# Values, up and down loaded in fewer or differently cut transfers at the end of a decode step

## The chip, the core and the metric

The kernel runs on one core of one Trainium2 chip. The metric is the device time of one execution in microseconds. Five engines work beside each other, each through its own queue of instructions in order: TensorE (PE: matmuls, and PEld: the loads of its stationary operand), VectorE (DVE), ScalarE (ACT), GpSimd (POOL) and SyncE (SP), which here does nothing but issue transfers from main memory. Sixteen DMA engines carry those out.

## What is computed

One decode step of a transformer block, for a single token of width 640, with 32 heads of 128 and a cache of 16384 positions per head:

```
mod = silu(c) @ w_mod                       # sa, ca, ga, sb, cb, gb: 640 each
h = layernorm(x) * (1 + ca) + sa
q = h @ wq                                  # 32 heads of 128
p = softmax(q . k_cache / sqrt(128))        # per head, over 16384 positions
x = x + ga * ((p . v_cache) @ wo)
h = layernorm(x) * (1 + cb) + sb
x = x + gb * ((silu(h @ w_gate) * (h @ w_up)) @ w_down)     # 640 -> 1728 -> 640
```

All inputs are bf16. The two caches are 128 MiB each in bf16, so nearly all of the bytes are keys and values.

## The kernel before

**Heads in pairs.** The 32 heads go as 16 pairs. A pair's keys (8192 KB) lie in one half of `kring`, 64 KB in each of 128 partitions; its values lie in `vbuf`, only the last pair's values in the first half of `kring` (`v_at`, line 482). VectorE multiplies keys by the query and folds the products (lines 540 to 562), TensorE adds up the rest against an identity matrix (line 530, or 570 for the first and last pair), ScalarE takes exponentials (588), and TensorE multiplies by the values (504, one matmul per four positions of a partition).

**Transfers.** `dma` (line 79) puts a transfer on SyncE's queue; SyncE issues it when its dependencies are met, in program order. Within a transfer each partition's bytes are one contiguous run of main memory. A later step waits for a transfer by name. The lists of cut points say how a tensor is divided into transfers, and the steps that use it are divided at the same points: `VCUT` for the last pair's values (line 481; used in `load_v` and `pv`), `WCUT` for wo's heads (625; used in the transfers and in `project`), `UK` for w_up's five slices (638; steps `up0` and `up1`), and `NB` blocks of 512 rows, plus a short one, for w_down (227 and 642).

**The tail.** After the last pair's scores (`o_R[15]`) the second half of `kring` is free, and w_gate, w_up and w_down are loaded there, in this order, behind the last values and wo, which went out earlier. On TensorE, in this order, stand: the last pair's exponentials' sum, its values (`pv`, `diag`), the heads' column form (`am`), wo (670), the columns (682), the second layer norm's two sums (380, 389) with gate's first slice between them, gate's other four slices (`gate`), a row form of x (726), up (704 again), and down (751). Between them VectorE and ScalarE do the small steps: layer norm, silu, the product gate x up (`gu`, line 740), and after down the last two operations (755, 756) and two stores.

**Columns of gate and up, rows of down.** w_down's 1728 rows are spread over partitions, so that one matmul contracts 128 of them. In a block of 512 rows, partition p holds rows 4p to 4p + 3: chunk j of the block is every fourth row. The short block has 192 rows on 96 partitions, two each. Gate's and up's outputs must stand in that same order. `chunk(j)` gives for each of the 14 chunks the columns of w_gate and w_up, a slice with that step, and `f_gu` (line 699) loads them as the stationary operand of a matmul with a moving operand of one or two columns: 14 matmuls per slice of 128 inputs, 70 for up and 70 for gate.

```
def chunk(j):
    return (slice(512 * (j // 4) + j % 4, 512 * (j // 4) + 512, 4), 128) if j < 4 * NB else (slice(512 * NB + j % 4, F, 2), FR)
...
last = e.matmul(ps_t[0:w, n * j:n * j + n], lhsT=wv[:, k, cols], rhs=src[:, n * k:n * k + n], ...)
```

Down takes the 14 chunks in order, four matmuls each (one for each quarter of the 640 outputs, side by side in the array), and accumulates all in one bank: the first chunk starts the sum, the last stops it. Each of the four `down` steps waits for the product `gu` and for its own transfer.

Of the kernel before, what the change touches and what calls it, by code (L numbers as in the profile page):

```python
# [37 lines left out]
class _Plan:  # L38
# [34 lines left out]
    def op(self, eng, fn, deps=(), name="", chan=None):  # L73
        o = _Op(eng, fn, list(deps), name, len(self.ops), self.loop.get(eng), chan)
        o.sig = chan is not None
        self.ops.append(o)
        return o

    def dma(self, out_ap, in_ap, key, deps=(), name="", eng="sp", noncontig=False):
        nc = self.nc  # L80

        def fn(e, out_ap=out_ap, in_ap=in_ap, noncontig=noncontig):
            if noncontig:
                with nc.allow_non_contiguous_dma(reason="tiny vector layout change"):
                    return e.dma_start(out_ap, in_ap)
            return e.dma_start(out_ap, in_ap)  # L86

        return self.op(eng, fn, deps, name, chan=self.dma_chan(key))
# [126 lines left out]
def build(nc, A_x, A_k, A_v, A_wq, A_wo, B_wg, B_wu, B_wd, c_in, w_mod, out):  # L215
    H, S, Dh = A_k.shape[1], A_k.shape[2], A_k.shape[3]
    D = A_x.shape[2]
    F = B_wg.shape[1]
    assert Dh == 128 and D % 128 == 0 and S == 128 * 128 and H == 32
    KC = D // 128  # L220
    NP = H // 2
    T2 = 2 * S // 128
    NCH = T2 // 4
    SCALE = float(Dh) ** -0.5
    EPS = 1e-5
    NB = F // 512
    FT = F - 512 * NB
    assert FT % 2 == 0 and FT // 2 <= 128
    FR = FT // 2
    FCH = 4 * NB + 2  # L230
    QW = 32
    QR = 16
    RW = D // 4
# [3 lines left out]
    with es:  # L237
        block = es.enter_context(nc.Block())
        plan = _Plan(nc, es)
        op, dma = plan.op, plan.dma  # L240
        POOL, ACT, DVE, PE = "pool", "act", "dve", "pe"

        def sb(name, shape, dtype):
            return es.enter_context(nc.sbuf_tensor(name, list(shape), dtype))
# [10 lines left out]
        wu_v = kb[:, KC * F:2 * KC * F].rearrange("p (k n) -> p k n", k=KC)  # L255
        wd_v = kb[:, 2 * KC * F:2 * KC * F + FCH * D].rearrange("p (k n) -> p k n", k=FCH)

# [40 lines left out]
        h2_col = sb("h2_col", [128, KC], BF16)  # L298
        ab = sb("ab", [128, KC, 2], BF16)
        g_sb = sb("g_sb", [128, FCH], F32)  # L300
        eg = sb("eg", [128, FCH], F32)
        dg = sb("dg", [128, FCH], F32)
        rg = sb("rg", [128, FCH], F32)
        sg = sb("sg", [128, FCH], F32)
        gu_col = sb("gu_col", [128, FCH], BF16)
# [22 lines left out]
        u_ps = psb[1]  # L328
# [101 lines left out]
        def pick(half, n, o_m, free):  # L430
# [14 lines left out]
            deps=[o_m0, o_xn], name="t1")  # L445
# [11 lines left out]
        for g in range(H // 4):  # L457
            b = g % 2
# [9 lines left out]
            for half in range(2):  # L468
# [4 lines left out]
                    deps=[o_q[g]], name="qbc%d_%d" % (g, half)))  # L473
# [4 lines left out]
        d_k, d_v = [None] * NP, [None] * NP  # L478
        o_R, o_pv, o_exp, o_nb, o_mx, o_acc, o_ot = ([None] * NP for _ in range(7))
        KCUT = [0, T2 // 2, T2]  # L480
        VCUT = [0, 3 * T2 // 4, T2]
        v_at = lambda p: vbuf[:] if p < NP - 1 else kring[:, 0]

        def load_k(p):
# [5 lines left out]
        def load_v(p):  # L490
            deps = [o_R[NP - 2]] if p == NP - 1 else [o_pv[p - 1]] if p >= 1 else [o_q[-1]]
            cuts = VCUT if p == NP - 1 else [0, T2]
            d_v[p] = [dma(v_at(p)[:, a:b, :], v_src(p)[:, a:b, :], ("v", p == NP - 1, c), deps=deps, name="dma_v%d_%d" % (p, c))
                      for c, (a, b) in enumerate(zip(cuts, cuts[1:]))]

        def pv(p):
            cuts = VCUT if p == NP - 1 else [0, T2]
            prev = None
# [54 lines left out]
        def score_end(p, c, between=None):  # L553

            kv = kring[:, p % 2, KCUT[c]:KCUT[c + 1]]
            o = op(DVE, lambda e: e.tensor_tensor(  # L556
                out=kv, in0=kv, in1=qbc[:, p, :].unsqueeze(1).broadcast_to([128, KCUT[c + 1] - KCUT[c], 128]), op=ALU.mult),
                deps=[d_k[p][min(c, len(d_k[p]) - 1)]] + o_qev[p // 2], name="mult%d_%d" % (p, c))
            for i, w in enumerate((64, 32, 16)):
                if between and i < 2:  # L560
                    between[i]()
                o = op(DVE, lambda e, w=w: e.tensor_tensor(out=kv[:, :, 0:w], in0=kv[:, :, 0:w], in1=kv[:, :, w:2 * w], op=ALU.add),  # L562
                       deps=[o], name="fold%d_%d_%d" % (p, c, w))
            return o
# [43 lines left out]
        for p in range(1, NP - 1):  # L608
            plan.in_loop(("pe",), "pairs", (p - 1) // 2, NLOOP)
            if p >= FIRST:  # L610
# [8 lines left out]
        PL = NP - 1  # L619
        load_v(PL)  # L620
        f0 = score_end(PL, 0, before(PL))
        reduce_end(PL, 0, f0)
        pv(PL - 1)
        wo_src = A_wo.rearrange("(p k) n -> p k n", p=128)
        WCUT = [0, H // 2, 7 * H // 8, H]
        d_wo = [dma(wo_v[:, a:b, :], wo_src[:, a:b, :], ("wo", a), deps=[o_pv[PL - 1]], name="dma_wo%d" % a) for a, b in zip(WCUT, WCUT[1:])]
        diag(PL - 1)
        f1 = score_end(PL, 1)
# [6 lines left out]
        wdeps = [o_R[NP - 1]]  # L635
        d_wg = dma(wg_v, B_wg.rearrange("(p k) n -> p k n", p=128), "wg", deps=wdeps, name="dma_wg")
        wu_src = B_wu.rearrange("(p k) n -> p k n", p=128)
        UK = KC - 1
        d_wu = [dma(wu_v[:, 0:UK, :], wu_src[:, 0:UK, :], "wu0", deps=wdeps, name="dma_wu0"),
                dma(wu_v[:, UK:KC, :], wu_src[:, UK:KC, :], "wu1", deps=wdeps, name="dma_wu1")]  # L640
        d_wd = []
        for b in range(NB):
            d_wd.append(dma(wd_v[:, 4 * b:4 * b + 4, :].rearrange("p r n -> p (r n)"),
                            B_wd[512 * b:512 * b + 512, :].rearrange("(p r) n -> p (r n)", r=4), ("wd", b), deps=wdeps, name="dma_wd%d" % b))
        d_wd.append(dma(wd_v[0:FR, 4 * NB:FCH, :].rearrange("p r n -> p (r n)"),
                        B_wd[512 * NB:F, :].rearrange("(p r) n -> p (r n)", r=2), ("wd", NB), deps=wdeps, name="dma_wd%d" % NB))

# [1 line left out]
                 deps=[o_exp[PL], o_rz, o_onesf, o_rstd], name="L")  # L651
# [8 lines left out]
                  deps=[o_z, o_e32] + o_qev[-2], name="am")  # L660
        o_as = op(ACT, lambda e: e.activation(out=A_sb[:], in_=A_ps[:, 0:H], func=ACTF.Copy), deps=[o_am], name="as")

        def project(c):

            def f_wo(e):
                last = None
                for k in range(WCUT[c], WCUT[c + 1]):
                    r = k % 4
# [4 lines left out]
            return op(PE, f_wo, deps=[o_as, d_wo[c], o_exp[NP - 2]] + o_qev[-1], name="wo%d" % c)  # L673
        for c in range(len(WCUT) - 1):
            o_p = project(c)
        o_wr = [op(ACT, lambda e, a=a, b=b, ps=ps: e.activation(out=wo_row[:, a:b], in_=ps[:, 0:b - a], func=ACTF.Copy),
                   deps=[o_p, f1], name="wo_row%d" % a) for ps, a, b in ((wr_ps[0], 0, 512), (wr_ps[1], 512, D))]

        def f_cols(e):
# [9 lines left out]
        o_zu = op(DVE, lambda e: e.memset(u_ps[:, 0:FCH], 0.0), deps=[o_exp[NP - 1]], name="zero_u")  # L689
# [4 lines left out]
            deps=[o_ga, o_xf], name="x1")  # L694

        def chunk(j):
            return (slice(512 * (j // 4) + j % 4, 512 * (j // 4) + 512, 4), 128) if j < 4 * NB else (slice(512 * NB + j % 4, F, 2), FR)

        def f_gu(e, wv, ps_t, src, n, k0, k1):
            last = None  # L700
            for k in range(k0, k1):
                for j in range(FCH):
                    cols, w = chunk(j)
                    last = e.matmul(ps_t[0:w, n * j:n * j + n], lhsT=wv[:, k, cols], rhs=src[:, n * k:n * k + n],
                                    start=(k == 0 and j == 0), stop=(k == KC - 1 and j == FCH - 1), skip_group_check=True)
            return last
# [3 lines left out]
        def gate0(o_xc1):  # L710
# [6 lines left out]
            deps=[o_xc1, o_rstd1, o_onep_b], name="t2")  # L717
        o_h2 = op(DVE, lambda e: e.tensor_tensor(out=h2_col[:], in0=tt3[:], in1=sb_, op=ALU.add), deps=[o_t2], name="h2_col")
# [9 lines left out]
            return last  # L728
        o_xr = op(PE, f_xr, deps=[o_xsp, o_ot[PL], o_msk], name="x1_rows")
        o_x1r = op(ACT, lambda e: e.activation(out=x1_row, in_=xr_ps[:, 0:RW], func=ACTF.Copy), deps=[o_xr], name="x1_row")  # L730
        o_u0 = op(PE, lambda e: f_gu(e, wu_v, u_ps, h2_col, 1, 0, UK), deps=[o_h2, d_wu[0], o_zu], name="up0")
        o_u = op(PE, lambda e: f_gu(e, wu_v, u_ps, h2_col, 1, UK, KC), deps=[o_h2, d_wu[1], o_u0], name="up1")
        gp = g_ps[:, 0:2 * FCH].rearrange("p (j n) -> p j n", n=2)
        o_gt = op(DVE, lambda e: e.tensor_scalar_mul(out=sg[:], in0=gp[:, :, 0], scalar1=st[:, 7:8]), deps=[o_g, o_rstd1], name="gate_r")
        o_gs = op(DVE, lambda e: e.tensor_tensor(out=g_sb[:], in0=gp[:, :, 1], in1=sg[:], op=ALU.add), deps=[o_gt], name="gate_s")
# [4 lines left out]
        o_gum = op(DVE, lambda e: e.tensor_tensor(out=gu_col[:], in0=u_ps[:, 0:FCH], in1=sg[:], op=ALU.mult), deps=[o_sg, o_u], name="gu")  # L740

        prev = None
        for b in range(NB + 1):
            js = list(range(4 * b, min(4 * b + 4, FCH)))

            def f_down(e, b=b, js=js):
                last = None
                for j in js:
                    w = chunk(j)[1]
                    for r in range(4):  # L750
                        last = e.matmul(f_ps[32 * r:32 * r + 32, 0:RW], lhsT=wide(gu_col[0:w, j:j + 1]), rhs=wd_v[0:w, j, RW * r:RW * r + RW],  # L751
                                        start=(j == 0), stop=(j == FCH - 1), tile_position=(0, 32 * r))
                return last
            prev = op(PE, f_down, deps=[o_gum, d_wd[b], prev, o_nb[PL]], name="down%d" % b)
        o_t3 = op(DVE, lambda e: e.tensor_tensor(out=tt_row, in0=f_ps[:, 0:RW], in1=gb_row[:], op=ALU.mult), deps=[prev, o_gb], name="gb_ffn")
        o_or = op(DVE, lambda e: e.tensor_tensor(out=o_row[:], in0=tt_row, in1=x1_row, op=ALU.add), deps=[o_t3, o_x1r], name="o_row")
        o_dst = out[0, 0].rearrange("(r n) -> r n", r=4)
# [51 lines left out]
```

## Time and profile before

| | us |
|---|---|
| time, median of 3 runs | 681.06 (680.71 to 681.47) |
| the profiled execution's own time | 680.78 |
| its span, first to last instruction | 679.0 |
| TensorE busy | 365.4 (54%) |
| VectorE busy | 512.4 (75%) |
| ScalarE busy | 46.7 (7%) |
| main memory read | 290.47 MB, 428 GB/s over the span |

The profile is of one execution. Its instructions carry the number of the source line that issued them, the engine, the tensors written and read, their shape, and in brackets how long the engine had been idle before and what ended that. In such a row the first number is the start in microseconds from the start of the span, the second the time until the last of the merged instructions ends. In rows about a transfer the last number is the time from its issue by SyncE to the landing of its last byte. A window's row gives its bounds and length, the busy time and the count for PE and PEld, the share of full clock that TensorE was granted, the transfers' busy share and their rate.

### The profile page before, as it was taken

The numbers are of one execution on the slowest core, as the hardware profiler recorded it, in microseconds if no ns is written. First come the engines' busy times: TensorE is split into PE (matmuls) and PEld (weight loads), VectorE is DVE, ScalarE is ACT, GpSimd is POOL, SyncE is SP. The second block draws the span as 40 slices with busy tenths as digits, with TensorE's granted clock in tenths as the row PEclk, the third lists the DMA queues.
The fourth block names the chain that finished last, engine by engine and source line by source line (L and its number), as shares of the span: only waits on it lengthen the run. The fifth ranks groups of instructions, "written<-read, shape, count | busy, mean of one in ns | idle before, by whom it ended". The sixth has DMA issues, their size and how long they took to land.

```text
span 679.0 us, 4923 instructions
## 1 busy us (share of the span) xinstructions
PE 365.4 (54%) x2075; PEld 143.7 (21%) x2075; DVE 512.4 (75%) x181; ACT 46.7 (7%) x147; POOL 0.7 (0%) x6
## 2 busy tenths in 40 slices
PE   2522284755638174754818275663718475571666
PEld 1111122221212122221302122221212222121236
DVE  2189997959596996959597895959598695959801
ACT  1120000100000000000000010000000000000010
POOL 0000000000000000000000000000000000000000
PEclk9675565655657575565757555575756556575775
DMA  8999999999999999999999999999999999999997
GB/s 374 441 460 432 432 432 430 432 429 432 432 429 432 440 432 432 432 432 432 436 432 432 432 432 432 432 436 432 432 432 432 432 432 432 432 433 431 415 432 289
DMA packets 6612, 290.59 MB, mean 428 GB/s; under 512 B 746, under 2 KB 748, under 8 KB 1484
## 3 DMA queue, kind: packets, MB, share of 16 engines
q1 hardware_dynamic: 6596, 290.48, 99.2%
q8 instruction: 6, 0.10, 0.1%
q14 instruction: 2, 0.02, 0.0%
q10 hardware_dynamic: 8, 0.00, 0.0%
HBM read 290.47 MB, written 0.00 MB: 428 GB/s over the span
## 4 chain that ended last, share of the span: by engine, by line
DMA 49%; DVE 30%; issue 12%; PE 8%; SPq 0%; DVEq 0%
DMA kring<-in_A_k_cache_dram 45%; DVE kring L540 10%; PE psb L530 7%; DVE kring L545 6%; DVE kring L556 5%; DVE kring L562 5%; DMA kring<-in_B_w_down_dram 4%; DVE kring L550 3%; PE psb L570 1%; SPq L86 0%; DVE pm L576 0%; DVE nb L584 0%; PE psb L751 0%; DVEq L187 0%; DVEq L540 0%
## 5 line engine op out<-in xcount | busy, mean ns | idle before, releaser
L540 DVE TENSOR_TENSOR kring<-kring,qbc 128x16384 bf16<-128x16384 bf16 x28 | 243.2, 8687 | 96.3 <-DMA kring<-in_A_k_cache_dram 96.3
L530 PE MATMUL psb<-kring,ident 128*128 128x256 bf16 x448 | 197.4, 607 | 119.2 <-DVE kring L550 119.2
L545 DVE TENSOR_TENSOR kring<-kring 128x8192 bf16<-128x8192 bf16 x28 | 123.7, 4420 | 0.5
L530 PEld LDWEIGHTS psb<-kring,ident 128*128 128x128 bf16 x448 | 51.7, 121 | 249.1 <-DVE kring L550 128.8
L504 PE MATMUL psb<-vbuf,PZ 128*8 128x512 bf16 x960 | 82.0, 516 | 0.0
L580 PE MATMUL psb<-d,bd_f 128*128 128x64 f32 x32 | 11.0, 447 | 122.7 <-ACT d L578 122.7
L550 DVE TENSOR_TENSOR kring<-kring 128x4096 bf16<-128x4096 bf16 x28 | 64.0, 2285 | 0.5
L556 DVE TENSOR_TENSOR kring<-kring,qbc 128x16384 bf16<-128x16384 bf16 x4 | 34.8, 8688 | 23.5 <-DMA kring<-in_A_k_cache_dram 23.5
L504 PEld LDWEIGHTS psb<-vbuf,PZ 128*8 128x8 bf16 x960 | 26.5, 109 | 60.1 <-issue 50.9
L570 PE MATMUL psb<-kring,ident 128*128 128x128 bf16 x64 | 14.5, 392 | 40.5 <-DVE kring L562 40.5
L580 PEld LDWEIGHTS psb<-d,bd_f 128*128 128x128 f32 x32 | 8.0, 311 | 124.9 <-ACT d L578 66.5
L562 DVE TENSOR_TENSOR kring<-kring 128x8192 bf16<-128x8192 bf16 (+2 forms) x12 | 31.7, 2644 | 0.3
L519 PEld LDWEIGHTS psb<-sel,acc_sb 128*128 128x128 f32 x128 | 28.5, 310 | 8.4 <-issue 4.3
L519 PE MATMUL psb<-sel,acc_sb 128*128 128x2 f32 x128 | 25.6, 322 | 1.4 <-ACT acc_sb L510 1.4
L510 ACT ACTIVATE acc_sb<-psb 128x512 f32<-128x512 f32 x16 | 9.6, 597 | 206.1 <-PE psb L504 206.1
L588 ACT ACTIVATE PZ<-psb,nb 64x256 bf16<-64x256 f32 x32 | 15.0, 469 | 64.8 <-DVE nb L584 64.6
L570 PEld LDWEIGHTS psb<-kring,ident 128*128 128x128 bf16 x64 | 7.4, 122 | 46.9 <-DVE kring L562 41.8
L578 ACT ACTIVATE d<-negid,pm 128x64 f32<-128x64 f32 x16 | 5.6, 348 | 155.5 <-DVE pm L576 155.5
L463 PE MATMUL psb<-vbuf,h_col 128*128 128x512 bf16 x40 | 11.6, 463 | 7.9 <-DMA vbuf<-in_A_wq_dram 7.9
L523 ACT ACTIVATE OT_sb<-psb 128x2 f32 (+1 forms) x16 | 2.8, 172 | 155.7 <-PE psb L519 155.7
L576 DVE TENSOR_REDUCE pm<-psb 128x1 f32<-128x256 f32 x16 | 6.7, 417 | 3.7 <-PE psb L570 3.7
L463 PEld LDWEIGHTS psb<-vbuf,h_col 128*128 128x128 bf16 x40 | 4.3, 116 | 15.5 <-DMA vbuf<-in_A_wq_dram 8.8
(96 smaller groups left out, 78.6 us busy)
## 6 DMA issues: line engine op xcount, KB each, us to landing
kring<-in_A_k_cache_dram SPq DMA_DIRECT2D x2, 4096.0 KB, 40.1
kring<-in_A_v_cache_dram SPq DMA_DIRECT2D x1, 6144.0 KB, 34.1
vbuf<-in_A_wq_dram SPq DMA_DIRECT2D x1, 5120.0 KB, 25.6
kring<-in_w_mod_dram SPq DMA_DIRECT2D x1, 4800.0 KB, 14.0
vbuf<-in_A_wo_dram SPq DMA_DIRECT2D x1, 2560.0 KB, 18.7
kring<-in_B_w_gate_dram SPq DMA_DIRECT2D x1, 2160.0 KB, 18.9
kring<-in_A_v_cache_dram SPq DMA_DIRECT2D x1, 2048.0 KB, 38.7
vbuf<-in_A_wo_dram SPq DMA_DIRECT2D x1, 1920.0 KB, 23.0
```

The lines of the kernel that those rows point to most:

```text
L463: last = e.matmul(q_ps[b][:, 0:512], lhsT=h_col[:, k:k + 1].broadcast_to([128, 128]), rhs=wq_v[:, k, g * 512:(g + 1) * 512], start=(k == 0 ...
L504: last = e.matmul(acc_ps[32 * s:32 * s + 8, :], lhsT=PZ[:, p % 2, j, :], rhs=v_at(p)[:, 4 * j:4 * j + 4, :].rearrange("p t d -> p (t d)"), ...
L519: last = e.matmul(OT_ps[:, 0:2], lhsT=acc_sb[:, 128 * i:128 * (i + 1)], rhs=sel[:, i:8:4], start=(i == 0), stop=(i == 3))
L530: last = e.matmul(S_ps[p % 2][:, 0:T2], lhsT=ident[:], rhs=kring[:, p % 2, :, d], start=(d == 0), stop=(d == QW + QR - 1))
L540: return e.tensor_tensor(out=kv4, in0=kv4, in1=q4, op=ALU.mult)
L545: o_f = op(DVE, lambda e: e.tensor_tensor(out=kv4[:, :, 0], in0=kv4[:, :, 0], in1=kv4[:, :, 1], op=ALU.add), deps=[o_m], name="fold%d_%d" ...
L550: return op(DVE, lambda e: e.tensor_tensor(out=lo[:, :, 0:QR], in0=lo[:, :, 0:QR], in1=lo[:, :, QR:QW], op=ALU.add), deps=[o_f], name="fol ...
L556: o = op(DVE, lambda e: e.tensor_tensor(out=kv, in0=kv, in1=qbc[:, p, :].unsqueeze(1).broadcast_to([128, KCUT[c + 1] - KCUT[c], 128]), op= ...
L562: o = op(DVE, lambda e, w=w: e.tensor_tensor(out=kv[:, :, 0:w], in0=kv[:, :, 0:w], in1=kv[:, :, w:2 * w], op=ALU.add), deps=[o], name="fol ...
L570: last = e.matmul(S_ps[p % 2][:, KCUT[c]:KCUT[c + 1]], lhsT=ident[:], rhs=kring[:, p % 2, KCUT[c]:KCUT[c + 1], d], start=(d == 0), stop=(d ...
L580: o_mx[p] = op(PE, lambda e: e.matmul(mx_ps[:, 0:64], lhsT=bd_f[:], rhs=d2[:], start=True, stop=True), deps=[o_d2, o_bd1, o_bd2, o_nb[p - ...
L588: o_exp[p] = op(ACT, lambda e, half=half, ps=ps: e.activation(out=PZ[ps, p % 2, :, 4 * half:4 * half + 4], in_=S_ps[p % 2][ps, 0:T2].rearr ...
```

## The change

Five lists are cut differently.

- The last pair's values go in one transfer in place of two (three quarters and one quarter), and their product in one step.
- wo goes in two transfers, 28 heads and 4, in place of three (16, 12 and 4).
- w_up goes in one transfer in place of two (four slices and one), and `up0` and `up1` become one step.
- w_down's blocks become: rows 0 to 1023 with 8 to a partition, rows 1536 to 1727 with 2 to each of 96 partitions, and rows 1024 to 1535 with 4 to a partition, in this order of chunks.
- w_down's transfers stay four: the whole first block, the whole short block, and the last block's first three rows of each partition and then its fourth. Down's steps follow: 8, 2, 3 and 1 chunks.

```
-    NB = F // 512
-    FT = F - 512 * NB
-    FCH = 4 * NB + 2
+    FT = F % 512
+    FR = FT // 2
+    FCH = 14
+    BLOCKS = [(0, 128, 8, 0), (1536, FR, 2, 8), (1024, 128, 4, 10)]
+    DOWN = [(0, 0, 8), (1, 0, 2), (2, 0, 3), (2, 3, 4)]
...
-        VCUT = [0, 3 * T2 // 4, T2]
+        VCUT = [0, T2]
...
-        WCUT = [0, H // 2, 7 * H // 8, H]
+        WCUT = [0, 7 * H // 8, H]
...
-        UK = KC - 1
-        d_wu = [dma(wu_v[:, 0:UK, :], wu_src[:, 0:UK, :], "wu0", deps=wdeps, name="dma_wu0"),
-                dma(wu_v[:, UK:KC, :], wu_src[:, UK:KC, :], "wu1", deps=wdeps, name="dma_wu1")]
+        d_wu = dma(wu_v, wu_src, "wu", deps=wdeps, name="dma_wu")
...
+        for i, (b, r0, r1) in enumerate(DOWN):
+            f0, w, n, j0 = BLOCKS[b]
+            d_wd.append(dma(wd_v[0:w, j0 + r0:j0 + r1, :], B_wd[f0:f0 + w * n, :].rearrange("(p r) n -> p r n", r=n)[:, r0:r1, :],
+                            ("wd", i), deps=wdeps, name="dma_wd%d" % i))
...
         def chunk(j):
-            return (slice(512 * (j // 4) + j % 4, 512 * (j // 4) + 512, 4), 128) if j < 4 * NB else (slice(512 * NB + j % 4, F, 2), FR)
+            f0, w, n, j0 = [b for b in BLOCKS if b[3] <= j < b[3] + b[2]][0]
+            return slice(f0 + j - j0, f0 + w * n, n), w
...
-        o_u0 = op(PE, lambda e: f_gu(e, wu_v, u_ps, h2_col, 1, 0, UK), deps=[o_h2, d_wu[0], o_zu], name="up0")
-        o_u = op(PE, lambda e: f_gu(e, wu_v, u_ps, h2_col, 1, UK, KC), deps=[o_h2, d_wu[1], o_u0], name="up1")
+        o_u = op(PE, lambda e: f_gu(e, wu_v, u_ps, h2_col, 1, 0, KC), deps=[o_h2, d_wu, o_zu], name="up")
...
-        for b in range(NB + 1):
-            js = list(range(4 * b, min(4 * b + 4, FCH)))
+        for i, (b, r0, r1) in enumerate(DOWN):
+            js = range(BLOCKS[b][3] + r0, BLOCKS[b][3] + r1)
...
-            prev = op(PE, f_down, deps=[o_gum, d_wd[b], prev, o_nb[PL]], name="down%d" % b)
+            prev = op(PE, f_down, deps=[o_gum, d_wd[i], prev, o_nb[PL]], name="down%d" % i)
```

In each row of four numbers in `BLOCKS` stand the first row, the partitions, the rows of a partition and the first chunk; in each of `DOWN` the block and the rows of each partition, from and to. In the kernel after, the loop's lines have numbers higher by 3 (530 is 533 there, 504 is 507), the tail's up to 682 the same ones, gate's and up's matmul is line 705, and down's is 751 as before.

More of the change, by code (lines that the diff above doesn't have):

```diff
@@ L225, in build @@
     EPS = 1e-5
-    NB = F // 512
-    FT = F - 512 * NB
-    assert FT % 2 == 0 and FT // 2 <= 128
+    FT = F % 512
+    assert F == 1536 + FT and FT % 2 == 0 and FT // 2 <= 128
     FR = FT // 2
-    FCH = 4 * NB + 2
+    FCH = 14
+    BLOCKS = [(0, 128, 8, 0), (1536, FR, 2, 8), (1024, 128, 4, 10)]
+    DOWN = [(0, 0, 8), (1, 0, 2), (2, 0, 3), (2, 3, 4)]
     QW = 32
@@ L637, in build @@
         wu_src = B_wu.rearrange("(p k) n -> p k n", p=128)
-        UK = KC - 1
-        d_wu = [dma(wu_v[:, 0:UK, :], wu_src[:, 0:UK, :], "wu0", deps=wdeps, name="dma_wu0"),
-                dma(wu_v[:, UK:KC, :], wu_src[:, UK:KC, :], "wu1", deps=wdeps, name="dma_wu1")]
+        d_wu = dma(wu_v, wu_src, "wu", deps=wdeps, name="dma_wu")
         d_wd = []
[L642 to L646, printed above, removed]
+        for i, (b, r0, r1) in enumerate(DOWN):
+            f0, w, n, j0 = BLOCKS[b]
+            d_wd.append(dma(wd_v[0:w, j0 + r0:j0 + r1, :], B_wd[f0:f0 + w * n, :].rearrange("(p r) n -> p r n", r=n)[:, r0:r1, :],
+                            ("wd", i), deps=wdeps, name="dma_wd%d" % i))
         o_L = op(PE, lambda e: e.matmul(misc[:, LS0:LS0 + H], lhsT=ones_f[:], rhs=rsz[:], start=True, stop=True),
@@ L742, in build, with f_down @@
         prev = None
-        for b in range(NB + 1):
-            js = list(range(4 * b, min(4 * b + 4, FCH)))
-            def f_down(e, b=b, js=js):
+        for i, (b, r0, r1) in enumerate(DOWN):
+            js = range(BLOCKS[b][3] + r0, BLOCKS[b][3] + r1)
+            def f_down(e, js=js):
                 last = None
```

## The prediction

> **What bounds the kernel now.** I read the page first. It says how full the memory stream is.
>
> ```profile
> span 679.0 us, 4923 instructions
> ...
> DMA  8999999999999999999999999999999999999997
> ...
> HBM read 290.47 MB, written 0.00 MB: 428 GB/s over the span
> ...
> DMA 49%; DVE 30%; issue 12%; PE 8%; SPq 0%; DVEq 0%
> ```
>
> The transfers run without a hole to the last slice and the bytes do not change, so no edit can gain much before the tail. Next I read the timeline of the last 15 us: it tells who waits for whom once the bytes run out.
>
> ```profile
> 665.75 0.64 PEld L704 LDWEIGHTS psb<-ab,kring 128*128 128x128 bf16 x14 [0.54 <-DVE ab L711]
> ...
> 666.55 2.48 PEld L704 LDWEIGHTS psb<-ab,kring 128*128 128x128 bf16 x56
> ...
> 669.05 0.76 PE L726 MATMUL psb<-acc_sb,msk 128*32 128x160 f32 x8
> ...
> 669.75 2.93 PE L704 MATMUL psb<-h_col,kring 128*128 128x1 bf16 x70
> ...
> 672.79 0.17 DVE L740 TENSOR_TENSOR gu_col<-psb,sg 128x14 bf16<-128x14 f32 x1 [1.80 <-PE psb L704]
> 673.01 1.32 PE L751 MATMUL psb<-kring,gu_col 128*32 128x160 bf16 x32 [0.34 <-DVE gu_col L740]
> ...
> 675.56 0.99 PE L751 MATMUL psb<-kring,gu_col 128*32 128x160 bf16 x24 [1.22 <-DMA kring<-in_B_w_down_dram]
> 676.60 0.33 DVE L755 TENSOR_TENSOR qbc<-psb,gb_row 128x160 bf16<-128x160 f32 x1 [3.64 <-PE psb L751]
> ```
>
> Two chains reach the end close together. The arithmetic one (gate, up, their product, down) arrives at down at 673.01 us. The transfers hold it: the last 24 of 56 down matmuls start at 675.56, when the third block of down has landed. Uninterrupted, the 14 chunks (133 ns apart, 0.107 the first) would put the last one's start at 673.01 + 0.107 + 12 x 0.1335 = 674.72; it was 676.20, so the arithmetic has 1.48 us of slack. Third, the transfers: issue and landing of the last ones.
>
> ```profile
> kring<-in_B_w_down_dram SPq DMA_DIRECT2D x3, 640.0 KB, 25.7
> kring<-in_B_w_up_dram SPq DMA_DIRECT2D x1, 432.0 KB, 23.2
> kring<-in_B_w_down_dram SPq DMA_DIRECT2D x1, 240.0 KB, 27.2
> ```
>
> One by one in the trace: wo lands at 653.60, 658.27 and 659.82; gate at 664.94; up at 669.05 and 670.10; down at 671.83, 673.56, 675.51 and 676.01.
>
> **The transfers, part by part.** Values, wo and up lose one transfer each; down stays at four. The trace's packet records price a merge: a value row goes as 49152 bytes in 1820 ns plus 16384 in 615, where the other pairs' 65536 take 2422, so 13 ns less, times 8 rows per engine, 0.10 us. On the same slope wo gains 0.10 and up (516 + 135 against gate's 644) 0.06. Down costs by my estimate 8 x (385 + 150 + 55) against 8 x 3 x 196 ns, 0.01 more. Sum: the stream ends about 0.25 us earlier, near 675.76. A price per transfer beyond its packets does not show: the last 2048 KB of the values land 4.89 us after the part before, 429 GB/s, as in the stream. The bound below is -0.25; above, the 96-row block moving into the middle could disturb its neighbours. In the trace packets took about 1.7 times as long between 673.0 and 674.3, while that block's packets ran beside the block before; if that comes on top a second time it is some 0.6 us later.
>
> Waits that grow longer: the last values' product waits for all of them (647.50, starts 649.66: 2.2 us of cover, and behind it on TensorE stands the whole tail). The first wo step waits for 28 of 32 heads (658.27 before, about 0.2 earlier now; A_sb is there at 658.38): cover 0.1 to 0.3 us, the thinnest, and a lateness there moves all that follows. Up waits for 670.10 less 0.25. Without the next part up would start at 669.85 instead of 669.74; with it the wait is covered. SyncE issues each later transfer up to 0.47 us sooner, into a queue that is full anyway (the last down issue took 2.85 us waiting for room): nothing.
>
> **The step that is easily missed: weight loads.** The 1024 rows of down now lie 8 to a partition, so gate's and up's columns for those eight chunks are read with a step of 8 elements, 16 bytes, not 4 elements. Four chunks keep 8 bytes, the short two their 4. Every gate and up matmul loads a stationary operand, and TensorE is on the path from 665.75 to 672.68. How does the step price a read? Rows with other steps:
>
> ```profile
> 562.71:564.84 2.13, 2.13 (x5) 0.57 (x6) 1.00 1.14 492
> 586.00:592.92 6.92, 6.92 (x16) 1.86 (x16) 0.50 1.01 436
> ...
> 656.01 1.05 PE L519 MATMUL psb<-sel,acc_sb 128*128 128x2 f32 x8 [0.71 <-ACT acc_sb L510]
> ...
> 661.68 2.36 PE L682 MATMUL psb<-ind,qbc 128*128 128x1 f32 x10 [0.88 <-ACT qbc L676]
> ...
> 7.64 0.47 PEld L367 LDWEIGHTS psb<-ones_bf,qbc 1*128 1x128 bf16 x10 [7.64 <-issue]
> ```
>
> The first two are windows of line 530 (time, then PE busy, count, granted clock): 256 columns with a step of 256 bytes take 0.43 us at either clock, 1.67 ns each, where line 504's contiguous 512 columns, four streams at once, pass at 0.83 ns at half clock. Line 519 loads f32 weights packed, 112 ns apart; line 682, at the same clock, with a step of 20 bytes, 220 ns apart. Line 367 loads bf16 in four groups of 32 columns with a step of 10 bytes, 40 ns apart; gate and up, the same form with 8 bytes, 33.3 ns (60 such and 10 short ones of 80 ns make the 2.8 us of up). One estimate fits all: 1.67 ns for each 16-byte piece of memory that 32 columns touch, plus 6.7. At 8 bytes that is 16 pieces, 33.3 ns; at 10 bytes 20, 40 ns; at 16 bytes 32 pieces, 60 ns. I take 60. The low end is 33.3 (no effect), the high end 220 (the four groups read one after another, as line 682's 128 columns); 60 is nearest because line 367 has the very form of load and follows the fit.
>
> [...]
>
> Sum on TensorE, half clock granted throughout (0.50 in both windows of line 704). Per group of 14 chunks: 8 x 60 + 4 x 33.3 + 2 x 80 = 773 ns, before 12 x 33.3 + 160 = 560: +0.213. Gate's first group +0.21, its other four +0.85, up +1.07: 2.13 us, 80 loads x 26.7 ns. TensorE is in order, so the second layer norm sum behind the first group also comes 0.21 later and h2 at about 668.03; up starts at 669.74 + 1.07 = 670.81, long after. Silu's chain on VectorE and ScalarE ended 1.7 us before the product and now has more room. So the product ends at 675.09, and down starts at 673.01 + 2.13 = 675.14.
>
> By then the 1024 rows are in (about 673.3), and the later blocks come before their turn: 14 chunks 133 ns apart put the short block at 676.21, three rows at 676.47 (landing about 675.3), the last row at 676.87 (about 675.8). Down runs without a break; its last chunk starts 675.14 + 0.107 + 12 x 0.1335 = 676.85, in place of 676.20. Everything behind is unchanged: **+0.66 us**. So 2.13 of new work, less the 1.48 of slack that it uses up, and the earlier stream is worth nothing. The profiled execution, 680.78 around a span of 679.0, becomes 681.44; it lies 0.28 under the median of 681.06, so the median becomes **681.7**.
>
> **Rivals.** First: the loads do not feel the step. Then the last landing decides, at about 675.76, with one chunk behind it (0.05 + 0.34) instead of six: down ends at 676.15, not 676.57: -0.42, 680.4 profiled, 680.6 as a median. Against it stand lines 682 and 367; for it, that neither row has this very step. It decides while a load stays under 47 ns (80 x 13.6 ns are the 1.09 from 674.72 to a last chunk at 675.81).
>
> Second, the other way by more: the four groups of columns collide when they lie 512 bytes apart instead of 256. At 80 ns, the price of a short load, it is 80 x 46.7 = 3.73 us, of which 1.48 is absorbed: +2.25, 683.3; at 220 ns, 80 x 187 = 14.9 and 694.5. Against it: line 367's 320 bytes apart fit without any. From 69 ns on it is slower by over 0.2%.
>
> Third: the 96-row block in the middle holds up what follows, and the last landing decides after all. It must slip past 676.87, 1.1 us later than my sum, twice the disturbance seen: 0.6 us beyond that is 682.3.
>
> Fourth: each of the three removed transfers took a cost of its own with it that the packets don't show, and the stream ends over 1.5 us earlier, with the loads unslowed. Then the arithmetic alone sets the end, last chunk at 674.72: -1.48, 679.6. The 4.89 us between the two value landings speak against it. [...]
>
> **How the numbers follow.** Forecast 0.62; loads unslowed 0.15; loads slower than 69 ns 0.14; held-up transfers 0.06; cheaper transfers 0.03. The range 680.4 to 683.1 takes in the forecast (its own: 681.2 to 682.3, for 55 to 67 ns and the spread of the runs), the first rival and part of the second and third. About 0.2%, 1.4 us, is what a measurement of this kernel can tell from no change (its three runs span 0.11%). Over that slower: the second rival, half of the third and a tenth of the forecast, 0.24; faster: the fourth and a tail, 0.04; within: 0.72.
>
> **What would show it.** Up's 70 loads last 4.0 us instead of 2.93, the first gate group 0.74 instead of 0.52; 56 down matmuls in one run from about 675.1 with no wait for a transfer, and the chain of waits ends through up, not through down's landing. A down group that still waits for a transfer, or a group of 14 lasting 0.56 us, makes the forecast wrong.

## The result, and the profile after

The changed kernel takes 682.2 us (median of 22 runs, 681.0 to 684.0) where the kernel before takes 681.07 (median of 22, 680.7 to 682.2). The ratio is 1.0019, with a 95% interval of 1.0012 to 1.0026: slower by 1.1 us, clear of the noise by its interval, but just under the 0.2% that the prediction takes as the least that can be told from no change. The forecast was +0.66. The profiled execution took 682.16, its span is 680.4. Two times far above all others of their kernels, 722.21 and 944.04 us, are left out below.

The page after: span, transfers and the shares of the chain of waits by engine.

```profile
span 680.4 us, 4919 instructions
...
DMA  9999999999999999999999999999999999999996
...
HBM read 290.47 MB, written 0.00 MB: 427 GB/s over the span
...
DMA 48%; DVE 27%; issue 12%; PE 11%; DVEq 0%; SPq 0%; ACT 0%
```

The bytes and their rate are as before; TensorE's share of the chain went from 8% to 11%. The timeline of the tail after (line 705 is gate and up, 751 down, 670 wo):

```profile
657.45 0.20 ACT L661 ACTIVATE A_sb<-psb 128x32 bf16<-128x32 f32 x1 [0.91 <-PE psb L659]
...
658.10 3.41 PE L670 MATMUL psb<-vbuf,A_sb 128*32 128x512 bf16 x64 [0.68 <-DMA vbuf<-in_A_wo_dram]
...
666.45 0.94 PE L705 MATMUL psb<-ab,kring 128*128 128x2 bf16 x14 [0.46 <-DVE ab L712]
...
667.67 3.24 PE L705 MATMUL psb<-ab,kring 128*128 128x2 bf16 x56
...
671.54 4.07 PE L705 MATMUL psb<-h_col,kring 128*128 128x1 bf16 x70
675.72 0.17 DVE L740 TENSOR_TENSOR gu_col<-psb,sg 128x14 bf16<-128x14 f32 x1 [2.94 <-PE psb L705]
...
675.94 2.06 PE L751 MATMUL psb<-kring,gu_col 128*32 128x160 bf16 x56 [0.34 <-DVE gu_col L740]
678.05 0.33 DVE L755 TENSOR_TENSOR qbc<-psb,gb_row 128x160 bf16<-128x160 f32 x1 [2.16 <-PE psb L751]
```

Up lasts 4.07 us in place of 2.93, and down's 56 matmuls run without a break from 675.94, waiting for the product, not for a transfer. From the start of gate to the end of up it is 9.16 us, before 6.93: 2.23 more. Gate itself starts 0.70 later (666.45 for 665.75). Together 2.93, less the 1.48 of slack: 1.45, and the span grew by 1.4.

The 0.70 was not forecast. It arises ahead of gate, where the sum had no new work. Three windows of each profile, over the last values' product, over wo and over the columns (time; PE busy and count; the granted clock is the figure behind the five engines), before:

```profile
649.66:655.30 5.64, 5.64 (x65) 1.82 (x64) 0.36 (x1) 0.00 (x0) 0.00 (x0) 0.63 0.97 410
658.43:660.80 2.37, 2.36 (x64) 1.33 (x64) 0.00 (x0) 0.00 (x0) 0.00 (x0) 1.00 1.06 450
661.68:664.04 2.36, 2.36 (x10) 2.27 (x10) 0.00 (x0) 0.00 (x0) 0.00 (x0) 1.00 0.99 425
```

and after:

```profile
649.56:654.58 5.02, 5.02 (x65) 1.67 (x64) 0.36 (x1) 0.00 (x0) 0.00 (x0) 0.71 0.91 389
658.10:661.51 3.41, 3.41 (x64) 1.84 (x64) 0.00 (x0) 0.00 (x0) 0.00 (x0) 0.67 1.05 449
662.37:664.74 2.37, 2.37 (x10) 2.28 (x10) 0.00 (x0) 0.00 (x0) 0.00 (x0) 0.50 1.02 437
```

The stretch of full clock lay otherwise: it made the values' product 0.62 faster, but had run out during wo, at 659.25, so that the same 64 matmuls took 3.41 us at a mean clock of 0.67 instead of 2.37 at 1.00. And most of the product's gain was lost at once: A_sb was there at 657.65, but wo's first step waited until 658.10 for its 28 heads, which landed at 657.96. This wait comes from the change: in the kernel before, the first step needs 16 heads, which had landed at 653.60. What it is worth, a profile further below shows (up alone with the long step). The columns, f32 loads with a step of 20 bytes, take 2.36 us at a clock of 1.00 and 2.37 at 0.50: these loads did not follow the clock.

### The profile page after: what moved, and what is told of

It is laid out like the page before. It is cut to its first block, busy times and chain, and to the rows that moved or that the text cites. A ratio compares the mean times of both kernels' runs of the same rounds, so it can differ in the third digit from the quotient of the medians.

```text
span 680.4 us, 4919 instructions
## 1 busy us (share of the span) xinstructions
PE 365.1 (54%) x2074; PEld 146.4 (22%) x2075; DVE 512.5 (75%) x181; ACT 46.7 (7%) x147; POOL 0.7 (0%) x6
## 4 chain that ended last, share of the span: by engine, by line
DMA 48%; DVE 27%; issue 12%; PE 11%; DVEq 0%; SPq 0%; ACT 0%
DMA kring<-in_A_k_cache_dram 45%; DVE kring L543 10%; PE psb L533 7%; DVE kring L548 6%; DVE kring L559 4%; DMA vbuf<-in_A_wo_dram 3%; DVE kring L565 3%; DVE kring L553 3%; PE psb L705 1%; PE psb L507 1%; PE psb L573 1%; PE psb L670 1%; PE psb L682 0%; PE psb L751 0%; DVE pm L579 0%
```

## The experiments

Three theories were tried. **The reading step**: eight of fourteen chunks of gate and up are read with a step of 16 bytes, a load takes 60 ns instead of 33, and this costs what the slack does not cover. **The cuts**: the merged or reordered transfers make something wait. From the second group of runs on, **the moving slack**: the slack of 1.48 us belongs to the one execution that was profiled; where full clock comes otherwise, TensorE reaches gate up to 2.5 us later and there is none.

### The merges alone

The kernel before, with the values, wo and up cut as in the changed one:

```
-        VCUT = [0, 3 * T2 // 4, T2]
+        VCUT = [0, T2]
...
-        WCUT = [0, H // 2, 7 * H // 8, H]
+        WCUT = [0, 7 * H // 8, H]
...
+        d_wu = dma(wu_v, wu_src, "wu", deps=wdeps, name="dma_wu")
...
+        o_u = op(PE, lambda e: f_gu(e, wu_v, u_ps, h2_col, 1, 0, KC), deps=[o_h2, d_wu, o_zu], name="up")
```

> Only the merges: last values in one transfer, wo in two, up in one; down's blocks and their reading step stay as before. Theory of the reading step (gate's and up's loads with a step of 16 bytes take 60 ns and use up 1.48 us of slack): loads stay 33 ns apart, the stream ends about 0.25 us earlier, down's last six chunks follow it; ratio 0.9993 to 1.0003. Theory of the cuts (the longer waits of the merged transfers cost the time, above all wo's first step): at least half of the change's 1.1 us is here, ratio 1.0008 or more.

Measured: 680.91 us, ratio 0.9999 (0.9990 to 1.0007). On the kernel before, the merges cost nothing and gain nothing. Its profile caught an execution in which TensorE was late (681.69 us); the timeline shows what that does with loads of 33 ns (line 702 is gate and up there, 748 down):

```profile
668.22 0.72 PE L702 MATMUL psb<-ab,kring 128*128 128x2 bf16 x14 [0.46 <-DVE ab L709]
...
669.23 2.37 PE L702 MATMUL psb<-ab,kring 128*128 128x2 bf16 x56
...
672.22 2.92 PE L702 MATMUL psb<-h_col,kring 128*128 128x1 bf16 x70
675.47 2.06 PE L748 MATMUL psb<-kring,gu_col 128*32 128x160 bf16 x56 [0.34 <-DVE gu_col L737]
```

Gate starts 2.47 us later than in the profile of before, and down already runs without a wait for transfers. Of the 1.48 us nothing is left, with no change to any load.

### Down's blocks alone

The changed kernel, with the values, wo and up cut as before:

```
-        VCUT = [0, T2]
+        VCUT = [0, 3 * T2 // 4, T2]
...
-        WCUT = [0, 7 * H // 8, H]
+        WCUT = [0, H // 2, 7 * H // 8, H]
...
-        d_wu = dma(wu_v, wu_src, "wu", deps=wdeps, name="dma_wu")
+        UK = KC - 1
+        d_wu = [dma(wu_v[:, 0:UK, :], wu_src[:, 0:UK, :], "wu0", deps=wdeps, name="dma_wu0"),
+                dma(wu_v[:, UK:KC, :], wu_src[:, UK:KC, :], "wu1", deps=wdeps, name="dma_wu1")]
```

> Only down's new blocks, their order and their transfers, with gate's and up's columns read to match (step of 16 bytes for eight of fourteen chunks); values, wo and up are loaded in as many transfers as before. Theory of the reading step: gate and up together last 9.1 us instead of 6.9, down runs without a break, ratio 1.0007 to 1.002. Theory of the cuts: less than half of the change's time, ratio under 1.0008.

Measured: 683.14 us, ratio 1.0028 (1.0017 to 1.0039), above what the theory of the reading step gave. The whole loss is here. The seven times lie in two groups, 681.5 to 681.7 and 683.1 to 684.3.

### The reading step alone

The kernel before, with one line more in `f_gu`:

```
                     cols, w = chunk(j)
+                    cols = slice(j, 1024, 8) if j < 8 else cols
```

> The kernel before with one thing done: gate and up read the columns of their first eight chunks with a step of 16 bytes. No transfer changes. The products then stand in another order than down's rows, so that the output is not the reference's; the work is the same. Theory of the reading step: 80 loads at 60 instead of 33.3 ns, 2.13 us more on TensorE, 1.48 of it absorbed by the wait for down's third block: 0.65 us, ratio 1.0007 to 1.0014. Theory of the cuts: no change, ratio within 0.0003 of 1.

Measured: 683.32 us, ratio 1.0024 (1.0014 to 1.0035). No transfer changed, so the cuts are not needed to explain the loss: the columns' step does it alone. But the sum of 0.65 is too small. Again two groups: five times from 681.1 to 681.5, seven from 683.3 to 684.1. The profiled execution, 681.29, is of the first kind: gate starts at 665.50, gate and up last 9.17 us, the last down matmul ends 0.51 later than before. The forecast's sum is right for it; it is not right for the other seven.

### Four rows to a partition again

The changed kernel, with the first 1024 rows as two blocks in one transfer:

```
-    BLOCKS = [(0, 128, 8, 0), (1536, FR, 2, 8), (1024, 128, 4, 10)]
+    BLOCKS = [(0, 128, 4, 0), (512, 128, 4, 4), (1536, FR, 2, 8), (1024, 128, 4, 10)]
...
+                d_wd.append(dma(wd_v[:, 0:8, :].rearrange("p (b r) n -> p b (r n)", b=2),
+                                B_wd[0:1024, :].rearrange("(b p r) n -> p b (r n)", b=2, r=4), ("wd", i), deps=wdeps, name="dma_wd0"))
```

> The changed kernel with one thing undone: rows 0 to 1023 of down come in one transfer still, but as two blocks of 512 with 4 rows to a partition, so that gate's and up's columns are read with a step of 8 bytes again. All merges and the order of the blocks stay. Theory of the reading step: loads 33 ns apart, the whole loss goes, and the last landing with one chunk behind it sets the end: 0.3 to 0.5 us under the kernel before, ratio 0.9992 to 0.9996. Theory of the cuts: it stays slower than before, ratio over 1.0007.

Measured: 681.39 us, ratio 1.0003 (0.9995 to 1.0012). The loss goes, but the gain of 0.3 to 0.5 that the earlier stream and the short last transfer should have left does not come. The same kernel, profiled again:

> One more look at the changed kernel with 4 rows to a partition, whose first look was a late one (gate at 668.0, 681.4). Moving slack: another late one 681.1 to 681.6, an early one with gate before 666 and the last landing as the end, 680.6 to 680.8.

Measured: 681.44 us, an early one (gate at 665.82), and slower than expected for it. Its timeline says why (line 709 is up, 755 down):

```profile
670.05 2.93 PE L709 MATMUL psb<-h_col,kring 128*128 128x1 bf16 x70 [0.19 <-DMA kring<-in_B_w_up_dram]
674.75 1.52 PE L755 MATMUL psb<-kring,gu_col 128*32 128x160 bf16 x40 [1.77 <-DMA kring<-in_B_w_down_dram]
676.56 0.73 PE L755 MATMUL psb<-kring,gu_col 128*32 128x160 bf16 x16 [0.29 <-DMA kring<-in_B_w_down_dram]
```

Down waits 1.77 us for the 1024 rows: they land at 674.61, where before the second block of 512 had landed at 673.56. The last transfer lands at 676.92 (before 676.01; between 675.96 and 676.43 in the four profiles that have the transfers of before). So in this execution the transfers are not earlier by 0.25 us but later, by 0.5 to 0.9. In the first profile the last landing came at 676.06, but TensorE was late (gate at 668.02); its 681.42 us are no more than those of the early one. The third rival's mechanism is there; in the changed kernel it lies under the longer loads.

### Up alone with the long step

The kernel before, with the line for up only (`n` is 1 there, 2 for gate):

```
                     cols, w = chunk(j)
+                    cols = slice(j, 1024, 8) if j < 8 and n == 1 else cols
```

> The kernel before with only up (not gate) reading its first eight chunks' columns with a step of 16 bytes; the output is not the reference's. 40 loads by 26.7 ns are 1.07 us more on TensorE. Theory of a fixed slack of 1.48 us, as in the one profiled execution of before: all of it is absorbed, ratio within 0.0003 of 1. Theory of the moving slack (in some executions TensorE is granted full clock through wo and reaches gate at 665.8, in others half clock, and reaches it at 668.2 with no slack left): nothing lost in the first kind, about 1 us in the second, ratio 1.0003 to 1.001 and a wider spread than before. Theory that every load costs: ratio 1.0015.

Measured: 681.08 us, ratio 1.0006 (0.9997 to 1.0014). Seven times lie from 680.7 to 681.1, like the better ones of before; four from 682.4 to 682.7, about 1 us over the late ones of before (681.5 to 682.0). The same 1.07 us of work is free in one execution and, by these times, paid almost in full in another; no profile caught one of the four. The interval takes in 1, so the ratio alone does not exclude a fixed slack; the gap between the groups does.

The profile (680.97 us) is also a twin of the changed kernel's first one, with wo cut as before: the values' product took 5.03 us (5.02 there), and A_sb was there at 657.55 (657.65).

```profile
657.61 2.63 PE L670 MATMUL psb<-vbuf,A_sb 128*32 128x512 bf16 x64 [0.29 <-ACT A_sb L661]
...
665.20 0.72 PE L705 MATMUL psb<-ab,kring 128*128 128x2 bf16 x14 [0.46 <-DVE ab L712]
```

Here wo starts at once and takes 2.63 us, full clock lasts from 652.34 to 662.58 (in the changed kernel from 652.43 to 659.25), and gate starts 1.25 us earlier than there, though A_sb was only 0.10 earlier. So wo's merged transfer can cost time where the product is early, and the experiment with the merges alone could not show it, because there the slack lies behind such an execution. In the traces of the kernels before and after every stretch of full clock lasts 3.41, 6.83 or 10.24 us: one, two or three pieces of 3.41. Whether the wait itself cut the full clock short was not tried. It would fit the tails of all fourteen profiles: where the values' product and wo filled 1.41 us or more of a 3.41 us piece of full clock, another such piece followed; where they filled 1.25 or less, half clock did. Here they filled 1.56 of the piece that ends at 659.17, and 1.16 of the changed kernel's at 659.25.

### Further profiles of the changed kernel

Nothing is edited.

> The changed kernel once more, one look, for another profile of its tail. Theory of the moving slack: time follows the moment at which TensorE reaches gate; with full clock through wo and the columns 665.5 to 665.9 and a time of 681.1 to 681.6, with half clock in most of it about 668 and 683.3 to 684.0. Theory that the transfers make the two groups of times: late landings of gate, up or down instead.

Measured: 683.86 us. Its windows and its timeline:

```profile
649.75:656.24 6.49, 6.48 (x65) 2.01 (x64) 0.36 (x1) 0.00 (x0) 0.00 (x0) 0.55 0.92 390
659.35:663.19 3.84, 3.84 (x64) 1.84 (x64) 0.00 (x0) 0.00 (x0) 0.00 (x0) 0.60 1.01 432
664.08:666.44 2.36, 2.36 (x10) 2.28 (x10) 0.00 (x0) 0.00 (x0) 0.00 (x0) 0.87 1.01 432
```

```profile
668.16 0.95 PE L705 MATMUL psb<-ab,kring 128*128 128x2 bf16 x14 [0.46 <-DVE ab L712]
...
673.25 4.06 PE L705 MATMUL psb<-h_col,kring 128*128 128x1 bf16 x70
...
677.64 2.06 PE L751 MATMUL psb<-kring,gu_col 128*32 128x160 bf16 x56 [0.33 <-DVE gu_col L740]
```

The values' product took 6.49 us (5.02 in the first profile), wo 3.84 (3.41); gate starts at 668.16 and down at 677.64, with the last transfer in since 676.27. The landings hardly moved.

> A third look at the changed kernel. Moving slack: its time is the moment at which gate starts plus 15.7 us, within 0.2, as in its first two looks (666.45 and 682.16; 668.16 and 683.86), whatever that moment is, and no down matmul waits for a transfer.

Measured: 684.04 us, wo 4.47 us at a clock of 0.50, gate at 668.29. Gate's start plus 15.71, 15.70 and 15.75 us are the times of the three executions, and in none does down wait for a transfer. In these two late executions wo did not wait either: A_sb came after the 28 heads. What sets when full clock is granted was not tried and stays open.

### The price of a load

The kernel before, with other steps in `f_gu`:

```
                     cols, w = chunk(j)
+                    s = (1, 1, 6, 6, 6, 13, 13, 13)[j] if j < 8 else 0
+                    cols = slice(j, j + 128 * s - s + 1, s) if s else cols
```

> One look at the price of a load: the kernel before, its first eight chunks of gate and up read with steps of 2, 2, 12, 12, 12, 26, 26 and 26 bytes; the output is not the reference's. Theory of 16-byte pieces (1.67 ns for each piece that 32 columns touch, and no less than 0.83 ns a column, plus 6.7): 33.3, 46.7 and 60 ns. Theory that the step's length itself costs: 2 bytes under 33, 26 bytes well over 60.

Measured, as the distance between successive loads of up in the trace: 27 ns with a step of 2 bytes, 46 to 47 with 12, 58 to 60 with 26 (the kernel's own: 33 with 8, 60 to 62 with 16 in the changed kernel). The price by the estimate, 33.3, 46.7, 60 and 60 ns, holds at four steps (8, 12, 16 and 26 bytes), and the step of 26 bytes costs no more than that of 16. The floor was wrong: the packed load takes 27, not 33.3, so the estimate's 6.7 ns are not in it.

### The short block at full width

The kernel before, with rows 0 to 191 as the short block, the three others behind it, and all loads of 128 columns:

```
+            return (slice(FT + 512 * (j // 4) + j % 4, FT + 512 * (j // 4) + 512, 4), 128) if j < 4 * NB else (slice(j % 4, 256, 2), FR)
...
-                    last = e.matmul(ps_t[0:w, n * j:n * j + n], lhsT=wv[:, k, cols], rhs=src[:, n * k:n * k + n],
+                    last = e.matmul(ps_t[:, n * j:n * j + n], lhsT=wv[:, k, cols], rhs=src[:, n * k:n * k + n],
```

> The kernel before with its short block moved to the front of the 1728 rows, so that its gate and up loads can take 128 columns (the last 32 results unused) instead of 96; transfers keep number, size and order. 20 loads go from 80 to 33 ns if all loads of 128 columns run in four groups at a time: 0.93 us less on TensorE. Theory of a fixed slack: no gain, the transfers set the end, ratio within 0.0003 of 1. Theory of the moving slack: executions that were late gain up to 0.9 us, the others nothing; ratio 0.9993 to 0.9999 and a narrower spread.

Measured: 680.96 us, ratio 0.9997 (0.9988 to 1.0005), all eleven times between 680.7 and 681.2. The loads of 96 columns went from 80 to 27 ns, which takes 0.5 us off up (2.42 for 2.93 in the last experiment's timeline, with the same loads), and no late group is left in its times. With the short last transfer of the changed kernel it was tried too: four rows to a partition as above, wo in three transfers, all loads of 128 columns, and

```
-    BLOCKS = [(0, 128, 4, 0), (512, 128, 4, 4), (1536, FR, 2, 8), (1024, 128, 4, 10)]
+    BLOCKS = [(FT, 128, 4, 0), (FT + 512, 128, 4, 4), (0, FR, 2, 8), (FT + 1024, 128, 4, 10)]
```

> The changed kernel with its merges of values and up and its short last transfer, but with 4 rows to a partition everywhere, the short block at the front of the rows so that its loads take 128 columns, and wo in three transfers again. Against the experiment with 4 rows to a partition alone TensorE has 0.93 us less to do. Moving slack: late executions are now held by the transfers too; the last landing near 676.1 with one chunk behind it gives 680.6 to 680.8 in both kinds, ratio 0.9991 to 0.9997, spread as narrow as that of the wide loads alone. If the last transfers' disturbance by the block in the middle decides instead, ratio 0.9998 to 1.0004.

Measured: 681.16 us, ratio 1.0000 (0.9991 to 1.0009). The figure of the moving slack failed here: the 1024 rows land at 674.29, the last transfer at 676.62, and down waits 2.1 us for the two, after up had waited 1.15 us for w_up in one transfer. What TensorE saves, the transfers do not give.

### The short block on all partitions

The trace's packet records show where the transfers lose. Before, packets of 5120 bytes take 196 ns, but mostly 300 to 378 between 673.0 and 674.2, while 2560-byte packets of the 96-row block (102 ns alone) mostly take 160 to 215 beside them. In the changed kernel, where that block has a neighbour on both sides, there are two such stretches, 671.0 to 672.9 and 673.1 to 674.3.

The kernel with the short block at full width, with its transfer to 128 partitions in place of 96 (the last 32 are not used):

```
-        d_wd.append(dma(wd_v[0:FR, 4 * NB:FCH, :].rearrange("p r n -> p (r n)"),
-                        B_wd[0:FT, :].rearrange("(p r) n -> p (r n)", r=2), ("wd", NB), deps=wdeps, name="dma_wd%d" % NB))
+        d_wd.append(dma(wd_v[:, 4 * NB:FCH, :].rearrange("p r n -> p (r n)"),
+                        B_wd[0:256, :].rearrange("(p r) n -> p (r n)", r=2), ("wd", NB), deps=wdeps, name="dma_wd%d" % NB))
```

> The kernel with wide loads, with one line changed: the short block's transfer fills all 128 partitions, two rows each (256 rows, the last 64 of them loaded twice and not used), in place of 96. Theory of the uneven block (packets take 1.7 times as long whenever the transfer to 96 partitions runs beside another): no packet of down's transfers slows, the last landing comes near 675.6 in place of 676.0 to 676.5, although 82 KB more are read; ratio 0.9990 to 0.9996. Theory that down's matmuls, which read the same memory, slow the transfers: the slow stretch stays, and the extra bytes make it 0.1 to 0.2 us longer; ratio 0.9998 to 1.0003.

Measured: 680.61 us, ratio 0.9991 (0.9982 to 1.0000), times 680.4 to 681.3. No packet of down takes over 12% more than its kind any longer (5% for the 5120-byte ones), apart from two between 669.6 and 670.5, right behind a 16 KB fetch of instructions. Down's third block and the short one land at 675.07 and 675.86 (before 675.51 and 676.01), with 82 KB more to read. The timeline:

```profile
669.42 2.42 PE L704 MATMUL psb<-h_col,kring 128*128 128x1 bf16 x70
...
672.17 0.72 PE L751 MATMUL psb<-kring,gu_col 128*32 128x160 bf16 x16 [0.33 <-DVE gu_col L740]
...
673.57 0.72 PE L751 MATMUL psb<-kring,gu_col 128*32 128x160 bf16 x16 [0.67 <-DMA kring<-in_B_w_down_dram]
...
675.12 1.25 PE L751 MATMUL psb<-kring,gu_col 128*32 128x160 bf16 x24 [0.83 <-DMA kring<-in_B_w_down_dram]
```

Down's matmuls read the same memory at 673.57 while packets land unslowed (those of 5120 bytes within 5% of their kind): the uneven block slowed the transfers, not the matmuls. (In the changed kernel's first profile both slow stretches are over before down's first matmul at 675.94.) Why 96 partitions disturb was not tried. This version is 0.6 us under the kernel before by the medians and 1.6 under the changed one; its interval just reaches 1.

## Why the prediction was right or wrong

- **That it gets slower, by less than 0.2%, and through the loads: right.** The columns' step alone (1.0024) and down's blocks alone (1.0028) give the loss; the merges alone give none on the kernel before (0.9999).
- **The load at 60 ns: right.** 60 to 62 were measured; gate and up grew by 2.23 us, forecast 2.13. The price rose with the step: 27 ns packed, 33 with 8 bytes, 46 to 47 with 12, 60 with 16, and 58 to 60 with 26. The size came from lines 367 (40 ns with 10 bytes) and 682 (220 ns with 20). That a load reads four groups of 32 columns, in pieces of 16 bytes, was the author's estimate; the runs show 128 columns packed in 27 ns where 96 take 80, and no rise of the price from 16 bytes to 26.
- **Down without a break, ending through up: right**, in all three profiles.
- **"Less the 1.48 of slack that it uses up": wrong in size.** This is the failed term: +1.1 in place of +0.66. The slack was read off one execution with full clock through wo (2.37 us). In others wo takes 3.4 to 4.5 us and gate starts up to 2.5 us later; the profile of the merges shows such a tail with no slack at all. There the loads cost about their whole 2.1 us: the late group of the columns' step stands at 683.3 to 684.1, over late times of before at 681.5 to 682.0 (no profile caught the kernel before itself in one). Of the changed kernel's 22 times eight lie at 681.0 to 681.6, about 0.4 us over the early ones of before, and eight at 683.4 to 684.0, about 2 over the late ones. The median, 682.2, falls among the six between them, so that it came as near to the forecast as it did is partly luck of the mix. "Half clock granted throughout" was right for gate and up, but the row that mattered was wo's, ahead of them.
- **The thinnest cover, wo's first step: right to name, wrong to call covered.** The 0.1 to 0.3 us were read off the same one execution; with the product 0.62 us faster, wo started 0.45 us behind A_sb, 0.4 more than before. This belongs to the 0.70 of the result, and the twin with wo cut as before reached gate 1.25 us sooner. The profiled execution (682.16) is one of the six times between the groups; the two experiments that have the long loads and wo cut as before have none of their 19 times between 681.7 and 683.1. That fits wo's wait as the cause of the six, but the changed kernel with wo's cuts alone restored was not run.
- **"The stream ends about 0.25 us earlier": wrong, and hidden.** The last landing came at 676.12, 676.27 and 676.49 in the three profiles, not at 675.76, and the transfers of before end in the same stretch (675.96 to 676.43). The sum counted packets at their undisturbed price; the disturbance that the text noted at 673 to 674 was there twice. Under the long loads it costs nothing. Without them (four rows to a partition) the gain does not come: the first rival's 680.6 was not reached in any of eleven times with this order of blocks, 681.1 at the least.
- **The other rivals.** Loads that collide (second) and a cost per transfer (fourth): neither was found (60 to 62 ns a load, not 80 or 220; ratio 0.9999 for the merges alone). The third exists (last landings from 676.12 to 676.49) but does not decide in the changed kernel.

## What to carry to other kernels

A layout chosen for a transfer also sets the step with which another engine reads: price the loads of stationary operands by that step (here 27 ns packed, 33 with 8 bytes, 60 with 16), and try a narrow load at 128 columns where it is on the path (here 27 ns, where 96 columns took 80). Slack or cover read from one profile is that of one execution; look where its clock came from, or take several profiles, before work is charged against it. An experiment on a kernel with slack can hide a cost that a kernel without slack pays. A small transfer like the one to 96 partitions, beside which packets took about 1.65 times as long here, belongs where nothing waits, or on all 128, where all but two took at most 12% longer.

## What was not expected of the hardware

- A load of 128 bf16 columns with a step of 2 bytes (in the price of a load) or 4 (in the short block at full width) took 27 ns and one of 96 with a step of 4 took 80: 0.83 ns per column with 96 and 0.21, a quarter of that, with 128, as if the 96 went one after another and the 128 in four groups at once.
- The columns' ten f32 matmuls, whose loads have a step of 20 bytes, did not follow TensorE's clock: they took 2.36 to 2.37 us at 0.50, 0.87 and 1.00.
- Beside a transfer of 240 KB to 96 partitions, its neighbours' packets took about 1.65 times as long (median) for 1.2 to 1.9 us at a stretch; beside the same rows on 128 partitions they did not.
